# QK-normalised attention on one core: the norms' sums of squares on TensorE, four norm steps on GpSimd, and new planner lengths

## The chip, the core and the metric

The kernel runs on one core of a Trainium2 chip. The metric is device time in microseconds (us) of one execution. Engines: TensorE (PE, its weight loads PEld), VectorE (DVE), ScalarE (ACT), GpSimd (POOL) and SyncE (SP), which issues nearly all DMAs here. A difference of about 2% is what a measurement of this kernel can tell from no change.

## The reference

```python
B, H, S, D = 1, 32, 2048, 640
Dh = D // H                      # 20
# q, k, v: bfloat16 (1, 32, 2048, 20); t: bfloat16 (32,)
def reference(q, k, v, t):
    eps = 1e-6
    qn = q / (jnp.sqrt((q * q).sum(axis=-1, keepdims=True)) + eps)
    kn = k / (jnp.sqrt((k * k).sum(axis=-1, keepdims=True)) + eps)
    logits = jnp.einsum('bhqd,bhkd->bhqk', qn, kn) * t[None, :, None, None]
    attn = _softmax(logits, axis=-1)
    return jnp.einsum('bhqk,bhkd->bhqd', attn, v)
```

Each row of 20 numbers of q and k is divided by its norm; then comes ordinary attention for 32 heads. The product of the logits has 32 x 2048 x 2048 elements, all of which need an exponential.

## The kernel before

The 32 heads are worked off in 8 groups of 4 (`NH = 4`), and the 2048 queries of a group in 4 quarters of 512. One quarter of one group is a sub-block; there are 32. In a sub-block each of 4 heads has 16 blocks of 128 keys, so a sub-block has 64 tiles of 128 keys x 512 queries, and the kernel has 2048 tiles in all.

A tile goes one of two ways. On the ScalarE way its logits are made by TensorE in PSUM tile psA, two tiles at a time ("QKA"), and ScalarE takes the exponential of both in one ACTIVATE (L881). On the VectorE way the logits are made in psD ("QKD"), VectorE turns them into integers that are the bits of an approximate exponential (P1, L321; two adjoining banks in one instruction where both are full), and two shifted copies of them are made (shift copies, S1 and S2: L336 on VectorE for up to four tiles at once, L334 on GpSimd for one or two). TensorE then multiplies by v ("PV", L710): one matmul for a tile of the ScalarE way, four for a tile of the VectorE way. All PVs of a sub-block add up in psO; at its end VectorE drains psO (L356), takes reciprocals (L360), and the next sub-block's PVs may begin. While psO is not free, a QKA is written three times over (`mms * 3`), and at other times small "heat" matmuls on zeros (L554) fill TensorE.

psA has two slots of two banks, so that ScalarE works on one while TensorE fills the other; psD has 3 banks (`DBANKS = 3`).

The norms of a group are made while the group before it is worked on (`prep_ops`, fed by `feed_prep` along the progress of the group before). For groups 1 to 7 that is, for each half of the rows: the squares (sq, L256), their sums over 20 by a reduction (red, L259); then for all 128 sums of a partition at once an approximate inverse root (rs0 to rs5, L278 to L283), eps (L284), a reciprocal (inv, L285), all on VectorE; then GpSimd scales k and q by the result into kpad and qpad (L300), and SP issues two DMA transposes that make kT and qT (L410). Group 0 has its own start.

The order of all instructions is fixed ahead by a planner in the kernel's source (`make_plan`): it simulates the engines in steps of 5 ns with a planned length for each instruction, and each engine takes the instruction that is ready by that clock and has the lowest priority number. On the chip each engine runs its list in order and waits on semaphores of what an instruction needs. [...] The planner also decides how many tiles go each way: ScalarE takes tiles whenever a slot of psA is free, VectorE when a bank of psD is free.

## Time and profile before

| | |
|---|---|
| runs | 637.5, 647.54, 635.52 us (median 637.5) |
| profiled execution | 634.25 us, its span 632.5 us |
| busy in the span | PE 614.9, DVE 617.0, ACT 618.4, POOL 435.6 us |
| granted TensorE clock | 0.998 |
| exponentials (L881) | 666 instructions, 614.2 us busy |
| tiles on VectorE | 717 of 2048 |

How to read it: the span is from the first to the last instruction of the profiled execution; its own time is 1.75 us above the span. Busy time of an engine joins its instructions where they overlap, which they do: an ACTIVATE begins before the one ahead of it has ended. A line number is that of the instruction in the kernel before. TensorE's busy time counts matmuls from start to a modelled end, so that its share does not say that it is full. In rows of groups, the numbers behind the bar are the busy us, the mean ns of one instruction, and the idle us of the engine ahead of it with what ended it.

### The profile page before, as it was taken

How to read it: one execution, taken by the hardware profiler on the slowest of the kernel's cores; microseconds unless marked ns; L12 is line 12 of the kernel's file. 1: busy time of each engine (PE TensorE's matmuls, PEld its weight loads, DVE VectorE, ACT ScalarE, POOL GpSimd, SP SyncE). 2: the span in 40 equal slices, each digit the busy share in tenths (PEclk: the TensorE clock that was granted, in tenths of full speed). 3: DMA queues.
4: the chain of work that ended last, by engine and by line, in shares of the span. 5: the costliest groups of instructions: out<-in, count | busy, mean ns of one | idle time of the engine just before them, and what ended most of it. 6: DMA issues, size and time to landing. Idle time of an engine off the chain costs nothing.

```text
span 632.5 us, 16239 instructions
## 1 busy us (share of the span) xinstructions
PE 614.9 (97%) x6946; PEld 183.9 (29%) x6946; DVE 617.0 (98%) x873; ACT 618.4 (98%) x674; POOL 435.6 (69%) x552
## 2 busy tenths in 40 slices
PE   7999999999999999999999999999999999999995
PEld 3324222322223222332223232232222232222221
DVE  6899999999999999999999999999999999999996
ACT  7999999999999999999999999999999999999995
POOL 4577768576786577767667777776777766766672
PEclk9999999999999999999999999999999999999999
DMA  8400404022120313105021060220403102000000
GB/s 113 56 2 2 84 27 44 1 55 57 11 33 2 61 50 20 25 2 109 2 18 27 1 109 3 23 21 4 92 3 40 19 16 54 2 22 6 7 7 10
DMA packets 113774, 19.59 MB, mean 31 GB/s; under 512 B 102944, under 2 KB 113696, under 8 KB 113696
## 3 DMA queue, kind: packets, MB, share of 16 engines
q1 hardware_dynamic: 112896, 18.37, 19.2%
q8 instruction: 56, 0.92, 0.6%
q10 hardware_dynamic: 800, 0.12, 0.1%
q14 instruction: 22, 0.18, 0.1%
HBM read 7.87 MB, written 2.62 MB: 17 GB/s over the span
## 4 chain that ended last, share of the span: by engine, by line
ACT 57%; PE 36%; DVE 3%; DMA 1%; SPq 1%; issue 0%; POOL 0%
ACT pA L881 57%; PE psO L710 17%; PE psA L688 14%; PE psO L554 2%; PE psD L688 2%; DVE dI L321 2%; SPq L401 1%; DMA kT<-kpad 1%; DMA qk<-in_q_dram 0%; DVE dS L336 0%; DVE ssum L259 0%; DVE sqs L256 0%; DVE accT L356 0%; POOL kpad L300 0%; DVE vhalf L341 0%
## 5 line engine op out<-in xcount | busy, mean ns | idle before, releaser
L881 ACT ACTIVATE pA<-psA 128x1024 f16<-128x1024 f32 (+1 forms) x666 | 614.2, 1101 | 2.7 <-PE psA L688 1.3
L334 POOL TENSOR_TENSOR dS<-dI,shc 128x512 int32<-128x512 int32 (+1 forms) x439 | 363.5, 850 | 139.3 <-DVE dS L336 97.6
L321 DVE TENSOR_SCALAR dI<-psD 128x512 int16<-128x512 f32 x481 | 434.4, 938 | 3.4 <-PE psD L688 1.9
L688 PE MATMUL psA<-qT,kT 32*128 32x512 bf16 x1575 | 284.1, 383 | 7.3 <-ACT pA L881 4.4
L710 PE MATMUL psO<-pA,vaug 128*32 128x512 f16 (+1 forms) x1331 | 247.2, 384 | 0.6 <-DMA vaug<-in_v_dram 0.6
L710 PE MATMUL psO<-dS,vaug 128*32 128x512 f16 x1434 | 239.0, 384 | 0.0
L688 PE MATMUL psD<-qT,kT 32*128 32x512 bf16 x717 | 191.9, 383 | 1.2 <-DMA kT<-kpad 1.0
L710 PE MATMUL psO<-dI,vaug 128*32 128x512 f16 x717 | 161.6, 385 | 0.1
L710 PE MATMUL psO<-dI,vhalf 128*32 128x512 f16 x717 | 159.5, 385 | 0.0
L688 PEld LDWEIGHTS psA<-qT,kT 32*128 32x128 bf16 x1575 | 69.6, 91 | 244.9 <-ACT pA L881 227.2
L336 DVE TENSOR_SCALAR dS<-dI 128x2048 int16<-128x2048 int16 (+3 forms) x191 | 127.5, 675 | 0.0
L710 PEld LDWEIGHTS psO<-dS,vaug 128*32 128x32 bf16 x1434 | 55.7, 94 | 67.9 <-issue 50.7
L710 PEld LDWEIGHTS psO<-pA,vaug 128*32 128x32 bf16 x1331 | 54.2, 94 | 35.3 <-issue 27.4
L688 PEld LDWEIGHTS psD<-qT,kT 32*128 32x128 bf16 x717 | 45.2, 91 | 15.7 <-DVE dI L321 7.2
L710 PEld LDWEIGHTS psO<-dI,vhalf 128*32 128x32 bf16 x717 | 37.9, 94 | 25.6 <-issue 22.9
L710 PEld LDWEIGHTS psO<-dI,vaug 128*32 128x32 bf16 x717 | 37.7, 94 | 23.7 <-issue 12.6
L554 PE MATMUL psO<-zt 128*128 128x128 bf16 x432 | 39.4, 221 | 0.0
L362 POOL TENSOR_TENSOR ost<-accT,rec 128x320 bf16<-128x320 f32 x31 | 23.3, 750 | 15.4 <-DVE dS L336 8.6
L300 POOL TENSOR_TENSOR qpad<-qk,rn 128x320 bf16<-128x320 bf16 x31 | 21.9, 727 | 16.3 <-DVE dS L336 10.0
L300 POOL TENSOR_TENSOR kpad<-qk,rn 128x320 bf16<-128x320 bf16 x31 | 22.4, 737 | 15.2 <-DVE dS L336 10.5
L554 PEld LDWEIGHTS psO<-zt 128*128 128x128 bf16 x432 | 25.1, 97 | 23.4 <-issue 23.4
L259 DVE TENSOR_REDUCE ssum<-sqs 128x64 f32<-128x1280 bf16 (+2 forms) x19 | 24.0, 1263 | 0.1
(51 smaller groups left out, 97.6 us busy)
## 6 DMA issues: line engine op xcount, KB each, us to landing
vaug<-in_v_dram SPq DMA_DIRECT2D x32, 80.0 KB, 3.9
qk<-in_k_dram SPq DMA_DIRECT2D x7, 320.0 KB, 4.6
out_dram<-ost SPq DMA_DIRECT2D x28, 80.0 KB, 1.9
qk<-in_q_dram SPq DMA_DIRECT2D x6, 320.0 KB, 4.6
qk<-in_q_dram SPq DMA_DIRECT2D x4, 80.0 KB, 2.8
out_dram<-ost SPq DMA_DIRECT2D x7, 40.0 KB, 2.0
qk<-in_k_dram SPq DMA_DIRECT2D x1, 240.0 KB, 3.6
qk<-in_q_dram SPq DMA_DIRECT2D x1, 240.0 KB, 4.2
```

Of the source, the lines that this page charges most:

```text
L259: lambda e, o=o4, x=s4: e.tensor_reduce(o, x, AXIS_X, ALU.add),
L300: emit = lambda e, o=dst, x=src, s=sc: e.tensor_tensor(o, x, s, ALU.mult)
L321: lambda e: e.tensor_scalar(dst, psD[:, pb * QW:(pb + n) * QW], 1024.0 * LOG2E, 15360.0 - 1024.0 * LOG2K + SHIFTS[0], ALU.mult, ALU.add),
L334: lambda e: e.tensor_tensor(o.bitcast(I32), x.bitcast(I32), c, ALU.add), rd + ["shc"], wr)
L336: lambda e: e.tensor_single_scalar(o, x, float(SHIFTS[i] - SHIFTS[0]), ALU.add), rd, wr)
L362: pool_op("omul", 320, True, lambda e: e.tensor_tensor(dst, num, rcb, ALU.mult), [("accT", b), ("rec", b)], [("ost", ob, qg)]) if pool else
L401: ops.append(dma("ldv", lambda e, d=d_, s=s_: e.dma_start(d, s), [], [("v", b, hh)], 1.4, 4.0))
L554: return lambda e: e.matmul(bank, zt[:, 0:128], zt[:, 0:n], start=False, stop=False, skip_group_check=True)
L688: return lambda e: e.matmul(dst, lhsT, rhs, tile_position=(32 * hh, 0))
L710: return lambda e: e.matmul(dst, lhsT, rhs, start=first, stop=last, skip_group_check=True, tile_position=(0, 32 * hh))
L881: a = Op("ACT", "exp", lambda e, s=src, d=dst: e.activation(d, s, ACT.Exp), [("psA", slot)], [("pA", pslot, i) for i in range(WAVES[slot]) ...
```

## The change

For groups 1 to 7 the reductions leave VectorE. VectorE still makes the squares; two DMA transposes per group ("Ts", one for k, one for q, ten blocks of 128 each) bring them to `sqT`; TensorE multiplies each block with a 0/1 matrix `ind` (20 matmuls per group with 32 columns of output, in four steps of five) so that the 128 sums of a partition stand in a bank of psD, which is lent for that time. rs0 and rs1 read the sums from PSUM. rs2, rs3, rs4 and eps go to GpSimd. `ind` is made at the start by one GpSimd and two VectorE instructions. `next_bank` moves the rotation of the three psD banks past the one on loan. The planned lengths of GpSimd, ScalarE, TensorE and some VectorE instructions are changed, and so are several priorities and limits; the plan that comes out sends 726 tiles over VectorE.

```diff
-RUN_MIN = 4
+RUN_MIN = 3
-D_END = 4
-D_LAST = 14
+D_END = 6
+D_LAST = 18
-PREP1 = (.3, .35)
-PRIO = .9
-PRIO1 = 1
-DFIRST = 1
+PREP1 = (.25,.35)
+PRIO = 1.5
+PRIO1 = 0.8
+DFIRST = 2
-JOINB = 8
-POOL_MAX = 2
+JOINB = 6
+POOL_MAX = 3
-PVHOLD = (.2, .2)
+PVHOLD = (.22,.22)
-POOL0 = .19
+POOL0 = .145
+POOLL = .05
+ACT0 = .05
+ACT1 = .24
+PEL = .17
-PSLACK = .1
+PSLACK = 0.2
-SOON = 2
+SOON = 1.2
-DJOIN = .4
+DJOIN = 0.3
+NST = .1
+NSWAIT = 0.4
+NSP = 5
+NORM_POOL = ('rs2', 'rs3', 'rs4', 'eps')
...
-            return Op("POOL", name, emit, reads, writes, cost=c, lat=c + 0.1)
+            return Op("POOL", name, emit, reads, writes, cost=c, lat=c + POOLL)
...
+            for a in (1, 0) if hg else ():
+                sq, x3 = sqs[a][:, :], qk[b][:, a, :, :, :].rearrange("p h r d -> p (h r d)")
...
+                ops.append(dve("sq", w_, R2, lambda e, o=sq, x=x3: e.tensor_tensor(o, x, x, ALU.mult), ...))
+                ops.append(dma("Ts", lambda e, o=dst, x=sq: e.dma_start_transpose(o, x), keys[:1], [("sqT", a)],
+                               0.58 + 0.17 * n_, 1.75 + 0.17 * n_))
...
-                ops.append(dve(nm, n, rate, emit, reads, writes, fix))
+                ops.append(pool_op(nm, n, rate != R2, emit, reads, writes) if pool and nm in NORM_POOL else
+                           dve(nm, n, rate, emit, reads, writes, fix))
...
-                add("rs0", lambda e: e.tensor_scalar(ri, s_.bitcast(I32), ...), [SS], [K("ri")], R2)
-                add("rs1", lambda e: e.tensor_tensor(rb, s_, y, ALU.mult), [K("ri"), SS], [K("rb")])
+                add("rs0", lambda e: e.tensor_scalar(ri, sums().bitcast(I32), ...), [SS], [K("ri")], R1 if hg else R2)
+                add("rs1", lambda e: e.tensor_tensor(rb, sums(), y, ALU.mult), [K("ri"), SS], [K("rb")])
...
-            add("inv", lambda e: e.reciprocal(rn_, ra), [K("ra")], RN[a0:a1], R1, n * 7 * R1)
+            add("inv", lambda e: e.reciprocal(rn_, ra), [K("ra")], RN[a0:a1], R1, n * 5 * R1)
...
+            def step_sums():
+                o = sums_todo[0]
+                for a in range(2):
+                    t_ = P.last_w[("sqT", a)]
+                    if t_.done is None or t_.done + SEML > now:
+                        return False
+                if "at" not in o:
+                    pb = next_bank()
+                    if not empty(pb):
+                        return False
...
+                mms = [lambda e, j=j: e.matmul(dst, sqT[:, (5 * g + j) * 128:(5 * g + j + 1) * 128], ind[:, 32 * j:32 * j + 32],
+                                               start=j == 0, stop=j == 4, skip_group_check=True) for j in js]
...
-                               0.064 + n_u * QW / 1200.0, 0.19 + n_u * QW / 1200.0)
+                               ACT0 + n_u * QW / 1200.0, ACT1 + n_u * QW / 1200.0)
...
+                if sums_todo and not 0 < wait < NSWAIT and step_sums():
+                    return True
...
-                pb = issued_d % DBANKS
+                pb = next_bank()
...
-                n = 2 if pb + 1 < DBANKS and left(d_sb) > 1 and empty(pb + 1) else 1
+                n = 2 if pb + 1 < DBANKS and issued_d % RING + 1 < RING and left(d_sb) > 1 and empty(pb + 1) else 1
```

## The prediction, made before the changed kernel was run

> **What bounds the kernel now.** I read the page's head first, for the share of each engine, and then the table by stretches, because an average over ramp and steady work can hide who is full in between.

> ```profile
> span 632.5 us, 16239 instructions
> ...
> PE 614.9 (97%) x6946; PEld 183.9 (29%) x6946; DVE 617.0 (98%) x873; ACT 618.4 (98%) x674; POOL 435.6 (69%) x552
> ```

> ```profile
> core 0: us, PE busy (x) PEld busy (x) DVE busy (x) ACT busy (x) POOL busy (x), PEclk, DMA share, GB/s
> 100.00:180.00 80.00, 79.41 (x905) 22.70 (x900) 79.78 (x109) 80.00 (x88) 55.76 (x70) 1.00 0.22 36
> ```

> In this stretch, one of the steady ones, ScalarE has no idle time (80.00 of 80 us) and VectorE almost none (79.78). TensorE's 79.41 is of another kind, because its matmuls overlap and wait in flight. So two engines are full at once, and the planner's division of the tiles is what holds them level: relief for one of them shows in the end time only as far as tiles move to it from the other. The chain that ended last, in order of time, tells which of the two paces the other:

> ```profile
> 293.00 16.60 ACT pA L881 x18
> 309.65 0.82 PE psA L688 x6
> ```

> For most of the time the chain is a run of ScalarE's exponentials, here 18 in a row; between two runs stand threefold QKAs (six matmuls) like this one, written when psO is being drained at the end of a sub-block. In the run the exponentials follow each other by (16.60 - 1.10) / 17 = 0.912 us, the 1.10 being the length of one:

> ```profile
> L881 ACT ACTIVATE pA<-psA x666: 677/1098/1284, 8.3 to 624.3; 128x1024 f16<-128x1024 f32 x166, 128x1024 bf16<-128x1024 f32 x1
> ```

> Over all of them it is (624.3 - 8.3) / 665 = 0.926 us. The 0.014 us between, 9 us in all, go mostly to the 32 ends of sub-blocks. Head (8.3) and tail (632.5 - 624.3 = 8.2) are fixed.

> **The change part by part.** All prices but those of DMAs and waits come from the groups of instructions, shapes kept apart:

> ```profile
> L881 ACT ACTIVATE pA<-psA 128x1024 f16<-128x1024 f32 x664 | 612.8, 1102 | 2.5 <-PE psA L688 1.1 <-PE psD L688 0.4
> L321 DVE TENSOR_SCALAR dI<-psD 128x1024 int16<-128x1024 f32 x236 | 286.0, 1212 | 2.3 <-PE psD L688 1.5
> ...
> L334 POOL TENSOR_TENSOR dS<-dI,shc 128x512 int32<-128x512 int32 x246 | 253.6, 1038 | 127.1 <-DVE dS L336 87.5 <-DVE sqs L256 14.4 <-DVE rsb L279 6.1
> ...
> L321 DVE TENSOR_SCALAR dI<-psD 128x512 int16<-128x512 f32 x245 | 164.8, 675 | 1.1 <-PE psD L688 0.4
> ...
> L336 DVE TENSOR_SCALAR dS<-dI 128x2048 int16<-128x2048 int16 x182 | 123.6, 686 | 0.0
> L334 POOL TENSOR_TENSOR dS<-dI,shc 128x256 int32<-128x256 int32 x193 | 117.6, 611 | 12.1 <-DVE dS L336 10.2 <-DVE rsa L284 0.8 <-DVE ssum L281 0.5
> ...
> L554 PE MATMUL psO<-zt 128*128 128x128 bf16 x432 | 39.4, 221 | 0.0
> ...
> L259 DVE TENSOR_REDUCE ssum<-sqs 128x64 f32<-128x1280 bf16 x14 | 20.6, 1470 | 0.0
> ...
> L311 POOL TENSOR_TENSOR rn<-rn,tb 128x64 f32<-128x64 f32 x7 | 2.1, 293 | 0.0
> L282 DVE TENSOR_TENSOR ssum<-ssum,rsa 128x128 f32<-128x128 f32 x7 | 2.0, 284 | 0.0
> L279 DVE TENSOR_TENSOR rsb<-ssum,rsi 128x128 f32<-128x128 f32 x7 | 2.0, 283 | 0.0
> L280 DVE TENSOR_TENSOR rsa<-rsb,rsi 128x128 f32<-128x128 f32 x7 | 2.0, 282 | 0.0
> ...
> L278 DVE TENSOR_SCALAR rsi<-ssum 128x128 int32<-128x128 int32 x7 | 1.6, 224 | 0.0
> ...
> L284 DVE TENSOR_SCALAR rsa<-rsb 128x128 f32<-128x128 f32 x7 | 1.5, 217 | 0.0
> L281 DVE TENSOR_SCALAR ssum<-rsa 128x128 f32<-128x128 f32 x7 | 1.5, 215 | 0.0
> ```

> *ScalarE.* 726 tiles on VectorE leave 2048 - 726 = 1322 for ScalarE, where there were 1331 (664 x 2, a pair in bf16, a single one). That is 4.5 pairs fewer at 612.8 / 664 = 0.923 us: **-4.15 us** on the engine that carries the chain. This is the only term that is on the path by the trace of before.

> *VectorE.* Gone: 14 reductions, 20.6 us; rs2, rs3, rs4, eps, 7 x (0.282 + 0.215 + 0.284 + 0.217) = 7.0 us; together 27.6. Added: rs0 reads f32 from PSUM, and I price it as rs1's row instead of its own, 7 x (0.283 - 0.224) = 0.4. Two small instructions that make `ind` at the start, between 0.22 and 0.68 each, taken at 0.3: 0.6. Nine more P1 at (286.0 + 164.8) / 717 = 0.63: 5.7. While a psD bank is on loan, P1 pairs fall apart: a pair is 1.212 and two singles 1.350, about three pairs in each of 7 groups: 2.9. Then the shift copies. A GpSimd tile costs (253.6 + 117.6) / 685 = 0.54 us there (246 x 2 + 193 tiles) and 123.6 / 728 = 0.17 on VectorE (182 copies of four). The 28 moved steps cost GpSimd about 0.40 each, on the line between 0.293 (64 elements, L311) and 0.611 (256 elements, L334); no row shows a GpSimd tensor_scalar of f32, so the bounds are VectorE's own 0.215 and the 0.611. That is 11.2 us (6.0 to 17.1), or 21 shift tiles (11 to 32) that go back to VectorE, with the 18 of the nine new tiles 39 x 0.17 = 6.6 (4.9 to 8.5). Sum: -27.6 + 0.4 + 0.6 + 5.7 + 2.9 + 6.6 = **-11.4 us** (-13 to -9.5) of VectorE's 617.0. It had to fall by 4.15 to keep pace with ScalarE, so some 7 us of slack come about: VectorE is not what ends last any more. Of the relief only the nine tiles reach the end time.

> *TensorE.* 140 matmuls with full weights, priced by the heat matmul, 39.4 / 432 = 0.091: 12.8 us (they are narrower, so between zero beyond the weight load and this). In 28 steps each also changes mode, about 0.24 (the second row here), 6.7 more. The 27 extra PVs are nothing beside 4199.

> ```profile
> PEld psA L688 <- ACT pA L881: 227.2, 558, 0.8
> PEld psO L710 <- issue: 113.6, 479, 0.4
> POOL dS L334 <- DVE dS L336: 97.6, 118, 2.3
> ```

> The cover is the 39.4 us of heat matmuls, which are there to be displaced, and the 227.2 / 558 = 0.41 us for which TensorE waits for ScalarE before a QKA. A step is 5 x 0.091 + 0.24 = 0.70 us, so one that stands right before a QKA makes it 0.3 us late; with all 28 so it would be 8 us. The planner keeps steps away from a slot that comes free within 0.4 us, so I take **+1 us** (0 to 8).

> *DMAs.* Fourteen more transposes on SP's queue, ten blocks each. The second one at the start of the kernel, of 12 blocks, shows what the size does.

> ```profile
> qT<-qpad SPq DMA_TRANSPOSE x1, 3.7
> ```

> Over all transposes of q, which are of 16 blocks but for that one, it is:

> ```profile
> DMA to landing us min/median/max: 3.7/4.4/5.8
> ```

> From 3.7 at 12 and 4.4 at 16, ten blocks land in 3.35 us; the plan counts on 1.75 + 0.17 x 10 = 3.45. So I take the sums to be no wait, with 5.8 as the upper bound. Where the squares are made, SP issues loads of v and the stores of the finished group, as here in group 2's preparation:

> ```profile
> 96.26 3.40 SPq L401 DMA_DIRECT2D vaug<-in_v_dram  x3
> 100.56 2.28 SPq L428 DMA_DIRECT2D out_dram<-ost  x4
> 102.88 0.55 SPq L401 DMA_DIRECT2D vaug<-in_v_dram  x1
> ```

> The added transposes pass through SP behind these, and the finished kT and qT have most of a quarter of the group's time to spare.

> [...] The longest idle of GpSimd is for VectorE's shift copies (97.6 us, 118 times); the list of waits shows none of VectorE for GpSimd, and VectorE's copies hardly stretch, 683 ns at the median and 891 at most:

> ```profile
> L336 DVE TENSOR_SCALAR dS<-dI x191: 327/683/891, 24.0 to 624.5; 128x2048 int16<-128x2048 int16 x182, 128x1536 int16<-128x1536 int16 x4, 128x1024 int16<-128x1024 int16 x4, 128x512 int16<-128x512 int16 x1
> ```

> By that I charge VectorE nothing for the 28 new GpSimd instructions. [...]

> *Lengths and limits.* They cost no instructions. What they bring is in the 726 and in the order, and is bounded by the rivals.

> **Sum:** 634.25 - 4.15 + 1.0 = **631.1 us** against the profiled execution. That one lies 1.3 us under the lowest and 3.3 under the median of the three runs shown (637.5), so for a run as they come I say **632**.

> **Rivals.**

> *A. The ends of sub-blocks get shorter.* RUN_MIN, SOON and D_LAST bring the last shift copies of a sub-block forward, and VectorE has slack for the drain. For it: the chain shows the loss there. Against: the threefold QKAs stay, and they are what the chain runs through. If half of the 9 us goes, 626.5; with all of it gone, 622.

> *B. The sums hold TensorE up.* TensorE works in order, so a sums step that waits for a late transpose holds every QKA and PV behind it, and then ScalarE. For it: the loads of v in the same stretch, and 5.8 us at the worst. Price: 5.8 - 3.45 = 2.35 late, less the 0.41 that TensorE waits anyway, in 7 groups: 13.6, so 644.7. Against: it needs the worst case each time.

> [...]

> *D. The change does not do what it says*: the plan gets its 726 tiles, but ScalarE follows a plan with nothing to spare in its lengths (0.05 + 1024 / 1200 = 0.903 us for an exponential in the new plan, where the trace has 0.912 in a run) and gaps open elsewhere that eat the 4 us: 635 to 638.

> **How the numbers follow.** Forecast 0.45 (628 to 635), A 0.22, B 0.10, C 0.11, D 0.12. The likeliest is the forecast, 632. The range reaches over half of A and D and to B and C's nearer parts: 622 to 644. Faster by over 2% needs about 622.5 and under, the far end of A: 0.10. Slower by over 2% needs 647 and over, the far ends of B and C: 0.08. The rest, 0.82, is within 2%, about what a measurement of this kernel can tell from no change.

> **What would show it right or wrong.** Right: some 661 exponentials near 610 us busy, ScalarE still idle for nothing between 20 and 580 us, VectorE's busy time under 610 with gaps that it did not have, no L259 group of 64 columns but the start's, heat matmuls well under 432. The threefold QKAs stand in the chain as before. Wrong by A: the distance from first to last exponential under 609 us, where it is 616 now. Wrong by B: waits of PE for DMA into sqT of over 0.5 us a group. [...] Wrong by D: waits of ACT for PE that add up to over 5 us.

## The result, and the profile after

The changed kernel is slower: 1.011 times the kernel before (95% interval 1.008 to 1.015, 14 runs of each; medians 644.0 and 635.1 us). The interval keeps clear of 1, but the difference is smaller than the 2% by which a measurement of this kernel tells a change from none. The ratio leaves out the four longest executions of the changed kernel and the longest of the kernel before; the profiled one (654.04 us, with a second loss at its start, below) is among them, so its stretches are used here and its total is not.

The page's head and the granted clock by fortieths of the span, the kernel after:

```profile
span 652.2 us, 15875 instructions
...
PE 631.2 (97%) x6784; PEld 177.9 (27%) x6784; DVE 612.9 (94%) x867; ACT 618.6 (95%) x669; POOL 441.4 (68%) x508
...
PEclk9997999999998799989999989997999979999998
```

The row of the clock in the kernel before:

```profile
PEclk9999999999999999999999999999999999999999
```

The number of exponentials came out as forecast, and so did VectorE's direction. But the clock row, all nines before, now has dips, and ScalarE and VectorE, full before (98% each), have gaps (95% and 94%). The groups (as before: busy us, mean ns, idle ahead):

```profile
L951 ACT ACTIVATE pA<-psA 128x1024 f16<-128x1024 f32 x660 | 613.4, 1096 | 21.5 <-PE psA L758 11.2 <-PE psD L758 9.9
L349 DVE TENSOR_SCALAR dI<-psD 128x512 int16<-128x512 f32 x262 | 174.1, 673 | 12.8 <-PE psD L758 12.5
L364 DVE TENSOR_SCALAR dS<-dI 128x2048 int16<-128x2048 int16 x160 | 114.7, 721 | 0.0
L584 PE MATMUL psO<-zt 128*128 128x128 bf16 x135 | 18.8, 278 | 0.0
L718 PE MATMUL psD<-ind,sqT 128*128 128x32 bf16 x140 | 8.1, 179 | 0.0
L312 POOL TENSOR_SCALAR rsa<-rsb 128x128 f32<-128x128 f32 x7 | 3.7, 530 | 4.0 <-DVE dS L364 3.7
L308 POOL TENSOR_TENSOR rsa<-rsb,rsi 128x128 f32<-128x128 f32 x7 | 3.3, 471 | 5.0 <-DVE dS L364 3.7 <-DVE rsb L306 1.1
L310 POOL TENSOR_TENSOR ssum<-ssum,rsa 128x128 f32<-128x128 f32 x7 | 3.2, 456 | 6.3 <-DVE dS L364 2.8 <-DVE dI L349 2.5 <-DVE rec L388 1.0
L309 POOL TENSOR_SCALAR ssum<-rsa 128x128 f32<-128x128 f32 x7 | 2.1, 300 | 2.1 <-DVE dS L364 1.7
```

ScalarE is now idle for 21.5 us ahead of its exponentials, nearly all for TensorE, where it was 2.5, and the single P1 wait 12.5 us for it. There are 135 heat matmuls, not 432. Where the waits are shows in a table by stretches around the sums of one group (busy us of PE, PEld, DVE, ACT, POOL, then clock, DMA share, GB/s):

```profile
194.00:204.60 10.60, 10.60 (x121) 2.79 (x113) 10.58 (x15) 10.60 (x13) 7.15 (x8) 1.00 0.42 82
204.60:208.50 3.90, 3.10 (x35) 1.27 (x31) 3.90 (x6) 3.90 (x6) 2.08 (x2) 1.00 0.02 4
208.60:218.80 10.20, 9.98 (x67) 2.06 (x67) 7.30 (x14) 7.70 (x9) 5.12 (x9) 0.50 0.00 2
218.80:229.00 10.20, 10.20 (x132) 2.70 (x128) 9.54 (x14) 9.93 (x12) 8.39 (x12) 1.00 0.01 2
```

In the second stretch stand the four sums steps: 35 matmuls in 3.9 us, 20 of them the short ones. In the third the clock is halved, TensorE gets through 67 matmuls where the next stretch of the same length has 132, and ScalarE makes 9 exponentials where that one has 12. TensorE's busy share there is 98%: at half clock a QKA's matmul lasts 0.61 us instead of 0.39 (below), which is why its share says nothing. The matmuls in order of time, across the same place:

```profile
205.15 0.39 PE L758 MATMUL psA<-qT,kT 32*128 32x512 bf16 x2 [0.19 <-ACT pA L951]
205.47 0.29 PE L718 MATMUL psD<-ind,sqT 128*128 128x32 bf16 x5
206.07 0.39 PE L758 MATMUL psA<-qT,kT 32*128 32x512 bf16 x2 [0.31 <-ACT pA L951]
...
207.90 0.39 PE L758 MATMUL psA<-qT,kT 32*128 32x512 bf16 x2 [0.31 <-ACT pA L951]
208.22 0.29 PE L718 MATMUL psD<-ind,sqT 128*128 128x32 bf16 x5
208.82 0.61 PE L758 MATMUL psA<-qT,kT 32*128 32x512 bf16 x2 [0.31 <-ACT pA L951]
```

For four of ScalarE's cycles TensorE does little beside a QKA and a sums step, and idles 0.2 to 0.3 us in each until ScalarE frees a slot. The five matmuls of a step fill 0.29 us with their tail of 0.18, so they start about 0.028 us apart; the plan booked 0.1 each, 0.5 a step, and put no PVs beside them. Then the matmul of a QKA goes from 0.39 to 0.61 us: the halved clock. The same follows the sums of six of the seven groups, for 3.4 to 10.2 us. In the one left out, the second, TensorE is as idle around the sums (busy for 2.99 of 3.90 us) and the clock held; nothing here shows why. Over the six, 34 intervals between exponentials add up to 15.0 us beyond the plan's 0.903 each (14.2 beyond the 0.926 of the kernel before). That is more than the 8.9 us between the medians.

### The profile page after: what moved, and what is told of

It is laid out like the page before. It is cut to its first block, busy times and chain, and to the rows that moved or that the text cites. A ratio compares the mean times of both kernels' runs of the same rounds, so it can differ in the third digit from the quotient of the medians.

```text
span 652.2 us, 15875 instructions
## 1 busy us (share of the span) xinstructions
PE 631.2 (97%) x6784; PEld 177.9 (27%) x6784; DVE 612.9 (94%) x867; ACT 618.6 (95%) x669; POOL 441.4 (68%) x508
## 4 chain that ended last, share of the span: by engine, by line
ACT 55%; PE 38%; DVE 6%; DMA 0%; issue 0%; POOL 0%
ACT pA L951 55%; PE psO L780 19%; PE psA L758 15%; DVE dI L349 4%; PE psD L758 3%; PE psO L584 2%; DVE dS L364 1%; DMA qk<-in_q_dram 0%; DVE accT L384 0%; DVE rn L313 0%; PE psD L596 0%; DVE ssum L284 0%; POOL kpad L328 0%; DVE rec L388 0%; DVE sqs L281 0%
## 5 line engine op out<-in xcount | busy, mean ns | idle before, releaser
L349 DVE TENSOR_SCALAR dI<-psD 128x1024 int16<-128x1024 f32 (+1 forms) x494 | 440.6, 925 | 23.6 <-PE psD L758 19.9
L362 POOL TENSOR_TENSOR dS<-dI,shc 128x512 int32<-128x512 int32 (+2 forms) x366 | 356.3, 988 | 144.6 <-DVE dS L364 114.9
L758 PE MATMUL psA<-qT,kT 32*128 32x512 bf16 x1534 | 291.3, 400 | 12.6 <-ACT pA L951 9.8
L780 PE MATMUL psO<-pA,vaug 128*32 128x512 f16 (+1 forms) x1322 | 231.1, 397 | 0.0
L780 PE MATMUL psO<-dS,vaug 128*32 128x512 f16 x1452 | 228.9, 398 | 0.0
L758 PE MATMUL psD<-qT,kT 32*128 32x512 bf16 x726 | 199.3, 397 | 0.3 <-DVE dI L349 0.2
L364 DVE TENSOR_SCALAR dS<-dI 128x2048 int16<-128x2048 int16 (+3 forms) x212 | 138.3, 661 | 0.1
L390 POOL TENSOR_TENSOR ost<-accT,rec 128x320 bf16<-128x320 f32 x31 | 23.3, 752 | 12.0 <-DVE dS L364 11.2
L384 DVE STREAM_TRANSPOSE accT<-psO 128x512 f32<-128x512 f32 x32 | 22.5, 704 | 2.6 <-PE psO L780 2.6
L584 PE MATMUL psO<-zt 128*128 128x128 bf16 x135 | 18.8, 278 | 0.0
L584 PEld LDWEIGHTS psO<-zt 128*128 128x128 bf16 x135 | 11.2, 121 | 14.7 <-issue 13.3
```

The source lines that it names most:

```text
L349: lambda e: e.tensor_scalar(dst, psD[:, pb * QW:(pb + n) * QW], 1024.0 * LOG2E, 15360.0 - 1024.0 * LOG2K + SHIFTS[0], ALU.mult, ALU.add),
L362: lambda e: e.tensor_tensor(o.bitcast(I32), x.bitcast(I32), c, ALU.add), rd + ["shc"], wr)
L364: lambda e: e.tensor_single_scalar(o, x, float(SHIFTS[i] - SHIFTS[0]), ALU.add), rd, wr)
L384: dve("drain", QW, R1, lambda e: e.transpose(aT[:, :, :].rearrange("p b d -> p (b d)"), psO[:, :]), ["psO"], [("accT", b)], 0.03),
L390: pool_op("omul", 320, True, lambda e: e.tensor_tensor(dst, num, rcb, ALU.mult), [("accT", b), ("rec", b)], [("ost", ob, qg)]) if pool else
L584: return lambda e: e.matmul(bank, zt[:, 0:128], zt[:, 0:n], start=False, stop=False, skip_group_check=True)
```

## The experiments

All ratios are to the kernel before on the same chip, with 95% intervals. Times "at full clock" are of executions whose mean granted clock is at least 0.995.

**1. Fill the sums steps with wide matmuls; the plan stays as it is.**

```diff
+                fill = psD[:, o["at"] * QW + 128:o["at"] * QW + 512]
+                mms += [lambda e: e.matmul(fill, zt[:, 0:128], zt[:, 0:384], start=True, stop=True, ...)] * 2
                 op = Op("PE", "sums", None, [("sqT", g // 2), "ind", "zt"], [("psD", o["at"])])
```

> The changed kernel with its plan untouched; each of the 28 sums steps only gets two more matmuls of 384 columns of zeros into the unused part of the bank on loan, about 0.3 us, so that TensorE really works in the 0.5 us for which the plan counts it as busy. Theory T (the sums steps are planned as 0.5 us of full use, last about 0.13 us, and keep heat matmuls away; the clock gate then halves TensorE's clock for 3.5 to 10 us behind them): granted clock back to 0.99 or more, no half-clock stretch behind the sums, and about 14 us gained (what ScalarE loses inside those stretches), so 628 to 632 us. Rival L (the shorter planned lengths leave TensorE too few heat matmuls everywhere, 135 for 432): clock stays under 0.98, 640 us or more. Rival W (the new waits between VectorE, GpSimd and TensorE lose the time): the clock may rise, the time stays at 638 or more.

Ratio 0.996 (0.989 to 1.004), 633.8 to 640.5 us. The six stretches are gone; around the sums of the same group:

```profile
202.60:206.50 3.90, 3.90 (x42) 1.46 (x39) 3.90 (x6) 3.90 (x6) 2.07 (x2) 1.00 0.02 4
206.60:216.80 10.20, 9.90 (x111) 2.75 (x113) 9.97 (x19) 10.20 (x13) 7.71 (x14) 1.00 0.01 3
```

ScalarE is back at 13 exponentials in 10.2 us. L falls, since the heat matmuls are still 135; W falls for the time lost behind the sums. But all four times stayed above the 628 to 632 us expected. The profiled execution (640.5 us) ran its first 41 us cold, as the profiled one of the changed kernel did; the other three have no profile. In both the record of the clock begins only at 41 us, and the lengths of matmuls tell it, which are there those of the halved clock (0.61 us above); between 20 and 40 us, the changed kernel's (in this experiment 28 of 604 ns) ahead of those of the kernel before:

```profile
L758 PE MATMUL psA<-qT,kT 32*128 32x512 bf16 x28 | 8.5, 603 | 0.0
```

```profile
L688 PE MATMUL psA<-qT,kT 32*128 32x512 bf16 x50 | 9.0, 383 | 0.1
```

Experiments 6 to 8 take that up.

**2. Book the sums as no use of TensorE.**

```diff
-                used_w.append((st, end, 0.25 * each * len(strips) / (end - st)))
+                used_w.append((st, end, 0.0 if op.name == "sums" else 0.25 * each * len(strips) / (end - st)))
```

> The changed kernel, but the planner counts a sums step as no use of TensorE, so that it may add heat matmuls of its own around it. T: clock 0.99 or more, heat matmuls in the stretches of the sums, 628 to 633 us. L: clock under 0.98 and 640 or more, since the thin heat elsewhere is left as it is. W: 638 or more whatever the clock.

Ratio 1.026 (1.017 to 1.036), clock 0.962, 136 heat matmuls, one more than without the edit, and half-clock stretches behind four of the seven groups' sums, one of 17.1 us, besides one at the start. The planner added no heat around the sums, so the part of T that blamed the count of use was wrong. By the planner's rules heat comes only where TensorE has nothing else planned, and with 0.5 us a step, a QKA and the changes of mode those cycles were probably full by its clock; experiment 5 bears on that.

**3. The sums back on VectorE, the rest as changed.**

```diff
-            for a in (1, 0) if hg else ():
+            for a in (1, 0) if hg and SUMS else ():       # SUMS = False
```

> The changed kernel with the sums of squares back on VectorE as reductions (20.6 us there), no added transposes, no bank on loan; the four norm steps stay on GpSimd, and the new lengths and limits stay. T: without sums steps no half-clock stretches, clock 0.99 or more, 630 to 637 us. L: clock 0.96 to 0.975 as in the changed kernel, 640 or more. W: in between, by how much of the waits hang on the sums.

Ratio 1.001 (0.993 to 1.009), 717 tiles, 311 heat matmuls, one half-clock stretch of 3.4 us at the start and none later. At full clock 638.4 and 638.6 us, above the 630 to 637 expected, against 634.2 and 634.7 of the kernel before. The dips belong to the sums, and without the sums the new lengths, limits and norm steps lose about 4 us together. In the profiled execution 2.4 us of that lie at the end: from the start of the last exponential on it takes 10.6 us (636.5 - 625.9), where the kernel before took 8.2.

**4. The sums and norm steps under all old lengths and limits.**

```diff
-POOL0 = .145
-ACT0 = .05
+POOL0 = .19
+ACT0 = .064
...
```

> The changed kernel (sums on TensorE, four steps on GpSimd) planned with all lengths and limits of the kernel before. T: the sums steps are still booked as 0.5 us of full use, so half-clock stretches stay behind them: clock under 0.985, 636 to 645 us. L: clock 0.995 or more, heat matmuls near 432 again, and 628 to 634 us. W: 636 or more with a full clock.

Ratio 1.017 (1.009 to 1.024), 647.1 to 659.2 us, above the 636 to 645 expected, clock 0.963, six half-clock stretches, all within or right behind sums, 177 heat matmuls. The new lengths are not what lowers the clock.

**5. The sums planned at their measured length.**

```diff
-NST = .1
+NST = .026
```

> The changed kernel with the sums matmul planned at 0.026 us instead of 0.1, which is the distance at which they start in the trace (five in 0.13 us). The plan then has 0.4 us more in each step for PV or QKD. Theory T2 (four cycles in a row in which TensorE has only a QKA and a short sums step leave it so idle that the gate halves the clock): PVs follow in the same cycle, clock behind the sums stays full, 629 to 636 us. Rival (the gate falls because the matmuls of the sums are narrow, whatever stands beside them, or because of the wait for the transposes): half-clock stretches behind the sums stay, 640 to 648.

Planned are 0.026 us; the trace of the changed kernel has 0.028. Ratio 0.994 (0.988 to 0.999); at full clock 630.7 to 631.3 us; the profiled execution has no half-clock stretch before the last PVs, 203 heat matmuls and 729 tiles. (One more execution has such a mean clock, at 642.9 us.) Around the sums of the same group PVs now follow in the same cycle, as T2 expected:

```profile
190.07 0.39 PE L758 MATMUL psA<-qT,kT 32*128 32x512 bf16 x2
190.39 0.42 PE L718 MATMUL psD<-ind,sqT 128*128 128x32 bf16 x10
190.73 0.40 PE L780 MATMUL psO<-pA,vaug 128*32 128x512 f16 x4
```

One number in the plan turns the change from slower to slightly faster.

**6. Fill with narrow matmuls instead of wide ones; the plan stays as it is.**

```diff
+                fill = psD[:, o["at"] * QW + 128:o["at"] * QW + 160]
+                mms += [lambda e: e.matmul(fill, zt[:, 0:128], zt[:, 0:32], start=True, stop=True, ...)] * 13
```

> The changed kernel with its plan untouched; each sums step gets 13 more matmuls of 32 columns of zeros into the unused part of the lent bank, about 0.33 us, as much time as the two wide ones in the first experiment. If it is idle time that lets the clock fall, the narrow ones cure it as the wide ones did: clock 0.985 or more, 633 to 638 us. If the gate looks at the columns streamed, 13 x 32 = 416 against 768 leave it short: half-clock stretches stay in most groups, clock 0.96 to 0.98, 640 or more.

Ratio 0.990 (0.984 to 0.996), five executions at full clock at 629.5 to 630.0 us, less than the 633 to 638 expected. The kernel before has 16 at full clock on that chip, at 633.2 to 634.5. (Each has one more with such a mean clock, at 641.3 and 640.9 us; perhaps they began cold ahead of the clock's record, which no profile shows.) The head and the clock row of the profiled one, with a single dip at the start, its exponentials, and the stretches around the sums of the same group as above:

```profile
PE 615.8 (98%) x7148; PEld 184.1 (29%) x7148; DVE 612.7 (97%) x867; ACT 615.2 (97%) x669; POOL 441.7 (70%) x508
...
PEclk9799999999999999999999999999999999999999
```

```profile
L953 ACT ACTIVATE pA<-psA 128x1024 f16<-128x1024 f32 x660 | 610.0, 1098 | 5.2 <-PE psD L760 2.7 <-PE psA L760 2.2
```

```profile
195.50:199.40 3.90, 3.90 (x80) 2.31 (x77) 3.90 (x6) 3.90 (x6) 2.08 (x2) 1.00 0.02 4
199.50:209.70 10.20, 9.90 (x119) 2.88 (x119) 9.98 (x19) 10.20 (x13) 7.73 (x14) 1.00 0.01 3
```

Behind the narrow matmuls the clock is 1.00, as it was behind the wide ones, though they stream about half the columns, 416 a step against 768. So it is not the columns streamed that count here; TensorE's idle time fits all three experiments, 1, 5 and 6: around the sums it was busy for 3.90 of 3.90 us in 1 and 6, and for 3.10 in the changed kernel. This is the fastest version found by its best times, faster than both kernels, though by less than 2% against the kernel before.

**7 and 8. More warming at the start,** of the changed kernel with the wide fill and of the kernel before.

```diff
-HEAT0 = 11
+HEAT0 = 16
```

> The changed kernel with the wide fill of the first experiment and 16 warming matmuls at the start for 11 (about 2 us more of them). The wide fill alone had its clock halved up to 41 us in the profiled run, which cost ScalarE some 10 us there. If the changed plan's start is what remains: full clock from before 12 us on, 628 to 632 us and a ratio of 0.985 to 0.992 to the kernel before. If the cold start is chance and no matter of the warming matmuls: no better than the wide fill alone, 633 to 640.

> The kernel before with 16 warming matmuls for 11: the control of the other. Its runs on the last chip lay at 634 to 642 us with clocks of 0.984 to 0.997, so it has the cold start in some of them. If more warming cures that: runs close together at 634 to 636. If not: the same spread, ratio 0.995 to 1.005.

Ratios 1.004 (0.999 to 1.010) and 1.006 (1.000 to 1.012). The changed kernel with the fill took 638.2 to 652.2 us, no better than in experiment 1. The kernel before with the longer warming has two kinds of execution still, five at 636.9 to 637.2 us and five at 643.3 to 643.6 with clocks near 0.986: more warming does not do away with the longer kind, and this plan is 3.6 us longer at full clock. Neither was the clean test that I meant: the later start changed the whole plan (718 tiles in 7, 714 in 8). In the kernel before, too, a loss comes and goes (of its 31 executions beside experiments 5 to 8, 16 lay at 633.2 to 634.5 us and 15 at 638.7 to 647.0, all but one of these with a clock under 0.99), so a lower clock in some executions needs no change to the kernel. That it is the same cold start is not shown, since none of those 15 was profiled. What decides it stays open.

**9. The kernel before without its heat matmuls.**

```diff
-                if in_use() >= HEAT or cur == NSB or not cur_free():
+                if True:
                     return False
```

> The kernel before without its heat matmuls (the threefold QKAs stay). The prediction counted these 39.4 us as free cover. If they hold the clock: half-clock stretches appear, in the stretches where the heat matmuls stood (the preparation of each group, the start), clock 0.93 to 0.975, 640 to 655 us. If they are spare: clock 0.99 or more and 630 to 635 us.

Ratio 1.043 (1.034 to 1.052), clock 0.908 in the profiled execution, eight half-clock stretches before the end: more than either expectation allowed. The plan has 714 tiles, nearly as before. The longest, with its neighbours:

```profile
120.00:126.00 6.00, 5.23 (x61) 1.36 (x57) 5.98 (x8) 6.00 (x8) 4.92 (x6) 1.00 0.01 3
126.70:150.60 23.90, 23.06 (x136) 4.43 (x136) 17.70 (x29) 17.42 (x18) 12.08 (x16) 0.50 0.00 1
150.60:180.00 29.40, 28.86 (x341) 7.79 (x339) 28.73 (x40) 28.95 (x33) 17.55 (x23) 1.00 0.28 59
```

The heat matmuls, 39.4 us of TensorE, are worth some 27 us of kernel time (medians of 668.9 and 641.7). They are no spare time.

**10. The narrow fill, with the four norm steps on VectorE.**

```diff
-NORM_POOL = ('rs2', 'rs3', 'rs4', 'eps')
+NORM_POOL = ()
```

> The changed kernel with the narrow fill that held its clock, and the four norm steps back on VectorE (7.0 us there by the rows of before). If these steps bring what VectorE's rows say: VectorE is full again and 1 to 3 us are lost, 630.5 to 633 at full clock against 629.5 with the steps on GpSimd. If their hand-offs cost as much as they free: the same or less, 627 to 629.5.

Ratio 1.012 (1.004 to 1.019). Neither expectation came about. The plan is another (723 tiles), and its profiled execution has a half-clock stretch of 17.1 us at 384 us, at no sums. Its one execution at full clock took 644.7 us, for which no profile speaks. What the steps on GpSimd are worth by themselves is left open.

**11. The narrow fill under all old lengths and limits.** The edit is that of experiments 4 and 6 together.

> The changed kernel with the narrow fill, planned with all lengths and limits of the kernel before. It sends 723 tiles over VectorE by the run without the fill, so by ScalarE's pairs 1.5 x 0.923 = 1.4 us more than the changed kernel: 630 to 632 at full clock if the new lengths and limits bring nothing else. If the shorter lengths gain by themselves: 633 or more here. If they lose (nothing to spare in them): 629 or less.

Ratio 0.987 (0.979 to 0.996); at full clock 630.2 and 630.7 us, where the kernel before had 635.5 in its one execution at full clock. The profiled execution has two half-clock stretches, 20.5 us at the start and 3.4 at 163 us, neither at sums. Within what these runs can tell, the old lengths do as well as the new ones once the clock is held.

## Why the prediction was wrong

*The step that failed* is TensorE's, "the cover is the 39.4 us of heat matmuls, which are there to be displaced", and with it the +1 us (0 to 8). I counted engine time, and by that the cover held: the sums took 8.1 us, less than the 12.8 charged, and where a QKA follows them it waits for ScalarE's slot, not for the step (0.31 us in the rows above). But the heat matmuls help to keep the clock full, as experiment 9 shows (0.908 without them), and a sums step that stands in the place of PVs is no stand-in, because its matmuls start 0.028 us apart and not 0.1. What lowered the clock is TensorE's idle time in these few cycles and not the smaller number of heat matmuls as such: experiment 1 has the same 135 and no dip. The loss is 15 us in the profiled execution, over six halved stretches (experiments 1 and 6 add matmuls to the sums steps alone, and the six are gone). None of my rivals was about the clock, and "heat matmuls well under 432" stood among the signs of being right. I had read the 0.998 as a state of affairs, while the 432 heat matmuls in the same profile said that it had to be held.

*ScalarE, -4.15 us:* right in size once the clock is held. At full clock the changed plan with the narrow fill takes 629.5 to 630.0 us against 633.2 to 634.5: 3.7 us less between the fastest, 4.5 between the slowest. That fewer exponentials bring it fits experiment 5, whose profile has no halved stretch among them: 660 of them, where there were 666, start within 610.0 us, where it was 616.0, so they are 0.926 us apart, as before. That its time fell by 3.5 us and not by 6 is due to the end: the tail that the forecast took as fixed was 10.5 us there (628.9 - 618.4) for 8.2.

*VectorE, -11.4 us:* mis-sized. Its busy time fell by 4.1 (617.0 to 612.9, over the 610 that was to show the forecast right), and with the clock held, in experiment 6, to 612.7. The shift copies cost more, 138.3 us in all for 127.5, where 6.6 more were forecast: a copy of four tiles went from 686 to 721 ns in the mean, and the longest copy from 891 to 1179:

```profile
L364 DVE TENSOR_SCALAR dS<-dI x212: 278/678/1179, 31.2 to 643.2; 128x2048 int16<-128x2048 int16 x79, 128x1024 int16<-128x1024 int16 x12, 128x1536 int16<-128x1536 int16 x11, 128x512 int16<-128x512 int16 x4
```

The 160 copies of four alone lose 160 x 0.035 = 5.6 us. The rest of the 7.3 us that were missed is not taken apart here. The median is unchanged, so a few wait long: 24 copies of four take over 750 ns, where one did before. Each of the 24 begins while a GpSimd instruction is running and ends 0.55 us after that one in the median, as here:

```profile
52.45 0.61 POOL L362 TENSOR_TENSOR dS<-dI,shc 128x256 int32<-128x256 int32 x1
52.61 1.01 DVE L364 TENSOR_SCALAR dS<-dI 128x2048 int16<-128x2048 int16 x1
```

So GpSimd held VectorE up in these places, and that is the case to which the forecast gives 0.11 as C. The prediction charged nothing for it, by the trace of before; but seven copies there, of 719 to 891 ns, also end 0.55 us after a GpSimd instruction beside which they began. Neither the median of VectorE's copies (683 ns before, 678 after) nor the list of waits, which has none of VectorE for GpSimd, shows it. The 5.6 us stay under the 7 us of slack that the prediction found for VectorE, so it did not decide. But the 28 moved steps are not what holds VectorE up: of the GpSimd instructions ahead of the 24, 20 are shift copies, three scale k or q, one is an output, and none is a moved step. Experiments 10 and 11 agree, the new limits with the steps on VectorE ahead of the old limits with the steps on GpSimd:

```profile
L364 DVE TENSOR_SCALAR dS<-dI 128x2048 int16<-128x2048 int16 x141 | 99.1, 712 | 0.0
L364 DVE TENSOR_SCALAR dS<-dI 128x2048 int16<-128x2048 int16 x168 | 115.4, 695 | 0.0
```

So most of it goes with the new limits. PSLACK, by which the plan lets a GpSimd instruction that begins beside one of VectorE's end up to 0.2 us after it, where it was 0.1, is the likely one, but no run changes it alone.

*GpSimd:* the four steps cost 3.7 + 3.3 + 3.2 + 2.1 = 12.3 us, 11.2 forecast.

*DMAs, rival B:* right that they cost nothing. Landing of the added transposes, and what TensorE waited for ahead of the matmuls that read them:

```profile
its engine sat idle before it (us, times) until:
  issue: 5.9, 26
  DVE dS L364: 0.5, 2
who waited for it (us, times):
busy tenths in 40 slices 0003000300003000030000300003000030000000
DMA to landing us min/median/max: 3.4/3.7/5.2
```

3.35 us was the estimate, 3.7 the median, and no wait of TensorE for a DMA is there.

*Rivals A and D:* the test of A (first to last exponential under 609 us) did not come about in the changed kernel (634.6 us), nor in experiment 5 (610.0). D's sign, ScalarE waiting over 5 us for TensorE, did appear (21.5 us), but from the clock and the cold start: with the clock held behind the sums the same wait is 5.2 us in experiment 6, in an execution that still has a halved stretch at its start, and 1.3 us in experiment 5, which has none.

## What to carry to other kernels

Where a filler on TensorE holds the clock, as here (0.998 with it, 0.908 without), it is work, not slack: before a change displaces it, ask how busy TensorE really is in each stretch of a few microseconds afterwards. A new kind of instruction in a planned order wants its measured length in both directions; one planned at 0.1 us that took 0.028 left gaps that no engine's busy share over the whole span showed. Look at the granted clock by stretches before explaining any wait: at half clock TensorE looks full (98% here), and the engines that wait for it look slow (9 exponentials of ScalarE in 10.2 us, and 12 at full clock).

## What the runs showed of the hardware

In the changed kernel 39 of VectorE's 160 copies of four tiles began while a GpSimd instruction still had 0.14 to 0.63 us to run; each ended 0.55 us after that one: with 0.29 us left a copy took 0.84, with 0.63 left 1.18. The 42 that began with 0.03 to 0.11 us left took 0.67 to 0.69, as did the 79 that began beside none.
